# A new fixed order for the opening of a linear-attention and expert kernel, with fourteen wide operations on other engines

## The chip, the core and the metric

The kernel runs on one core of a Trainium2 chip. A core has five engines with a queue of instructions each: TensorE (PE: matrix products and transposes through its array), VectorE (DVE), ScalarE (ACT), GpSimd (POOL) and SyncE (SP, which here only issues transfers). Within a queue instructions start in order; between queues they are held together by semaphores. The metric is the device time of one execution in microseconds (us). The profile is one further execution, recorded by the hardware.

## The reference

```python
q_s = softmax(q, axis=-1)            # over the 64 features
k_s = softmax(k, axis=2)             # over the 576 positions
kv  = einsum('bhsd,bhse->bhde', k_s, v)
x   = einsum('bhsd,bhde->bhse', q_s, kv)   # 8 batches, 8 heads, 576 x 64
x   = x.transpose(0, 2, 1, 3).reshape(4608, 512)
h   = x @ w_in                       # 512 -> 2048
r   = maximum(h, 0)
out = (s * (r * r) + b) @ w_out      # 2048 -> 512
```

Everything is float32. The two large products run as sums of products of a high and a low part of each operand (`x` and `xl`, `gh` and `gl`, two parts of each weight), three products where one stood.

## The kernel before

The 4608 rows of x are cut in blocks of 512. A block is worked off in 16 steps, one for each 128 columns of `w_in`. Step t needs the weights w(t), which arrive as float32 and are split into two parts ("conversion", `conv_w`, L296 to L330): ACT L307, DVE L311, ACT L314, DVE L318, ACT L323, DVE L326, in that order, on 1024 columns for most weights and on two halves of 512 for some. Then PE does twelve matmuls of `h` (L1468), ACT takes the positive part (L1500), DVE squares it (L1523), ACT adds b and rounds to `gh` (L1525), DVE makes the rest `gl` (L1527), and PE does twelve matmuls of `acc` (L1548), eight with `gh` and four with `gl`, the first three of them two with `gh` and one with `gl`. The 16 weights are converted once, during the first block; later blocks find them in place.

Before the first step some attention must be done. Heads go in pairs u = 0, 1, 2, ...; the first four fill the 512 columns of block 0. For a pair of k (`k_stream`, L432): PE turns it (`kT`, L440), DVE takes the maximum (`km`, L443), ACT the exponentials (L448), PE turns it back (`kn`, L453), and an engine named by `KN_ON` copies it to where it came from (L455). PE then makes `kv` (L402), and DVE scales it to `kvf` (L420). For a pair of q (`q_stream`, L508): DVE takes the maximum (`qm`, L519), DVE or POOL subtracts it (L522, by `SUB_ON`), ACT exponentiates (L528), DVE sums and inverts (L531, L533), DVE or POOL multiplies (L538, by `MUL_ON`), PE turns the result (`qT`, L543), ACT or DVE copies it (L546, by `QF_ON`), PE makes `xp` (L553), ACT rounds it to the high part of x (L559), and DVE makes the low part (L563). k of later pairs goes another way (`k_pair`, L457: DVE L621 to L625, PE L629, DVE L632, PE L636, DVE L640, ACT L647). Some results share a PSUM bank in turn: `kn`, `qT` and `xp` of the first four pairs have two banks between them, `h` has one.

Nothing in this is scheduled on the chip. Each of these chains is a stream of `Op` entries with an engine, a cost and what it needs; a planner (`Order`) takes one entry after the other, and the order in which it takes them is the order in each engine's queue. In the opening the planner does not choose: two letters of `TURNS_TAKEN` name the stream that goes next. Where PE would have to wait by the planner's costs, `idle` (L1691) puts idle transposes (`unused`, L1702) in its queue. Transfers are issued from SP in that same order, over eight semaphores in rotation, so that an issue waits until the eighth transfer before it has landed.

Of the kernel before, what the change touches and what calls it, by code (L numbers as in the profile page):

```python
# [26 lines left out]
def attention_moe(ctx: ExitStack, tc: tile.TileContext, q, k, v, w_in, w_out, s, b, out):  # L27
    nc = tc.nc
    B, H, S, D = q.shape
    DM, FF = w_in.shape  # L30
# [107 lines left out]
    TURNS_TAKEN = (
        "aaaaababaaaaabaaabaWabaWabaQaWaWabaQaWaQabaWaXaWaQabaXaRaQaWauaRaXabaXaWabaRaXaba8aRaXabaXavabaRabauaSavabaua8avaSabauabaSaYaoauaSa8aYaZaTaS"
        "aqauaWaYaZaYaTaXaWaYaTaZbcaYaWaYaZa9aTaXaZbcaXaTawaZaYaZaXa9awaYaXawavaZbcaZa9adbcawavaYadaxaZavaeaYaxaeacaZbcaYawaZbcbcacayawbcbcaye1axbdbc"  # L140
        "bda4bcaxbda4aybdbcafaxafa4aybdbcbdbcaxagbdbcagaUbcbdbeaUaybebda4beazayapbeaAbda4e2a4bdazbea4bdaAazbdbeaAa4bfazbfbeaAbfa4ahaza4ahbfbea4aiaDaU"
        "azbeaibfbeaDaAbebfbeaDaAbgbfbgaDe3aBbgaCbfbgakaDaBbfakaCa1bgbfaDaBbfaCbfbgaEbhaBbgbhaCbgaBbhajaCbhajaBbgaCbhe4a1bgaFbha1bga1aEbgbha1biaEbhbi"
        "a1bia1aGbiaEa1bibhaUalbiaFbhalaGbibha0bibha0a1aUbibja0aEaUbjaFaEbjbjaGaUbiaFaJbibjbiaJaUambjbiaJamaGbkbjbkaUaJanbkaFbjanbaa5aJaFa5aGbkarbaaK"
        "babjaJbaa5bjaKataGbjaKbkbjaKaHblbkaKblaHbkaKe5blaHbkblaIaHbkblaIbkaHblaIbkaHblbkaIe6a0bmblaIbma0asa5aIbmaNa0a1a0aLa5bma1a5aNblbma5a1blbmaVa0"
        "bmblaVbmblaLa0bnbmaNa0aNaLbna0bnaMa0bnaNaLa5bmaMbnaNbma5aLa5bnaMbma5aLbmbnaMe7boaObnboaMaOaPboaMaOaPboa2aPaVaObnboaVbnboaPaVboa2bnaVa2bnboaV"
        "bpaOaPbpboaVaObpaVaPbpe8a2a3bobpa2a3bobpa2boa2bpboa3bqbpa3a2bpbqa3a2bqa3a3bqbpbqeQeQbpbqbpbqbpbqa3bbbqa3brbbcubrbbbbbrcva2cwbra2bqa2brcxbqbr"
        "a3brbqbrbqa3brbsa3bsa6bsa7bsdgbrbsdgbrbsbrePdgdQbrbsdgePbtdQeQbtbtbseQbtdgdRdgbsbtbsdRbta6bsa7bta6bsbtbua7btbua6a7a6bua7a6a7bua6a7bta6bubta7"
        "bua6btbudgbta6budQa6bvdQbvdQbvdQbvbubvdQbubvdQbubvbubwbvdgbwbwdgdsbwdsa6bvdtcza7bwdtbva7bwdRbvbwa7dRbveea7e9bwbxe9dRbxfhdRdQbxfhefcydRfhbxdR"
        "efcBfhbwefbxbwfhefbxbwefdSbxbwfhdSbxfhbyfabyfhcCbyfibyfifhfibxbyfibxfidQbybxfadQbybxcAdhdSbzbybzdRdhbzdSbzdhdSbydhbzfbdSfibyerbzfibydhbzdSdh"
        "byerbzbAdSerbAfibAererdibAfifjbzdibAbzfjbAbzfbdTbAbzcDfjdRdTbAbBdRbBdhbBfjdTdibBdSfjdibAdTbBfcbAbBfjdTbAdifjdTdibAbBfjbCbBesdTfjbCbBesfkbCes"  # L150
        "bCdTfkesbBdhesbCfcbBfkbCdhbBdufkdUbBbCdufkbDdUdifkdvbDbCdvbDdSbCbDfkcEdSbCbDfkbCdUfdflbCbDflfkbCdUbDbEfldUbDflegdUdTflbDbEcFegbEflegflbEdieg"
        "bDbEdUegbDdwbEbDfddwflbEdUbDdicGbFbEdxbFflfmbFdxdVbFfmdVfmetbFfebEetbFbEfmbFetbEbFetbEetfmbGcHfmdTbGfmbGdTbGdVehfebGdVdUeSbGbFdVeSbGehcJbFdV"
# [1606 lines left out]
```

## Time and profile before

| | us |
|---|---|
| median of 3 runs (lowest, highest) | 827.82 (827.21, 828.38) |
| the profiled execution | 828.27 |
| its span, first to last instruction | 826.5 |
| PE, DVE, ACT, POOL busy | 817.6, 673.3, 463.5, 205.3 |

The profiled execution took 1.8 us more than its span and lies 0.45 us above the median. The granted clock of TensorE is 1.0 throughout, the higher of its two levels. A busy share over the whole span says little here: the opening of some 36 us, the rest of the first block to about 110 us, and all that follows have different limits, and the rows below are taken from each.

### The profile page before, as it was taken

The numbers are of one execution on the slowest core, as the hardware profiler recorded it, in microseconds if no ns is written. First come the engines' busy times: TensorE is split into PE (matmuls) and PEld (weight loads), VectorE is DVE, ScalarE is ACT, GpSimd is POOL, SyncE is SP. The second block draws the span as 40 slices with busy tenths as digits, with TensorE's granted clock in tenths as the row PEclk, the third lists the DMA queues.
The fourth block names the chain that finished last, engine by engine and source line by source line (L and its number), as shares of the span: only waits on it lengthen the run. The fifth ranks groups of instructions, "written<-read, shape, count | busy, mean of one in ns | idle before, by whom it ended". The sixth has DMA issues, their size and how long they took to land.

```text
span 826.5 us, 12888 instructions
## 1 busy us (share of the span) xinstructions
PE 817.6 (99%) x4301; PEld 676.7 (82%) x4301; DVE 673.3 (81%) x1155; ACT 463.5 (56%) x768; POOL 205.3 (25%) x206
## 2 busy tenths in 40 slices
PE   8999999999999999999999999999999999999997
PEld 7688888888888888888888888888888888888886
DVE  6999956799899996978979978699969976656883
...
GB/s 267 319 375 318 164 70 110 151 228 191 218 179 198 168 170 205 214 177 144 203 241 163 242 149 149 231 264 283 276 253 325 251 156 214 203 182 187 90 18 73
DMA packets 217206, 165.64 MB, mean 200 GB/s; under 512 B 91444, under 2 KB 200500, under 8 KB 217140
## 3 DMA queue, kind: packets, MB, share of 16 engines
...
q10 hardware_dynamic: 5024, 0.98, 0.6%
...
## 4 chain that ended last, share of the span: by engine, by line
PE 96%; DVE 2%; issue 1%; ACT 0%; POOL 0%; POOLq 0%; ACTq 0%
PE acc L1548 27%; PE h L1468 26%; PE bankU L1104 11%; PE overX L1195 8%; PE bankV L1104 8%; PE overY L1195 5%; PE overZ L1195 5%; PE xp L830 2%; PE kv L402 2%; PE kT L440 1%; PE xp L553 1%; PE unused L1702 0%; PE bankU L1195 0%; DVE low L318 0%; DVE st L311 0%
## 5 line engine op out<-in xcount | busy, mean ns | idle before, releaser
L1468 PE MATMUL h<-x,w 128*128 128x512 f32 x960 | 238.2, 392 | 1.3 <-ACT r L1500 0.8
L1468 PEld LDWEIGHTS h<-x,w 128*128 128x128 f32 x960 | 177.9, 188 | 38.8 <-ACT r L1500 1.3
L1548 PE MATMUL acc<-w,gh 128*128 128x512 f32 x640 | 199.2, 392 | 0.0
L1548 PEld LDWEIGHTS acc<-w,gh 128*128 128x128 f32 x640 | 118.1, 188 | 23.5
L1548 PE MATMUL acc<-w,gl 128*128 128x512 f32 x320 | 125.1, 391 | 0.1
L1500 ACT ACTIVATE r<-h 128x512 f32<-128x512 f32 x80 | 47.9, 599 | 94.7 <-PE h L1468 94.1
L1104 PE MATMUL bankU<-w,ring 128*128 128x512 f32 x378 | 95.9, 389 | 0.0
L1104 PEld LDWEIGHTS bankU<-w,ring 128*128 128x128 f32 x378 | 70.9, 188 | 14.7
L1548 PEld LDWEIGHTS acc<-w,gl 128*128 128x128 f32 x320 | 60.1, 188 | 14.2 <-DVE gl L1527 0.9
L1104 PE MATMUL bankV<-w,ring 128*128 128x512 f32 x282 | 71.5, 389 | 0.0
L759 POOL TENSOR_TENSOR qe<-qe,qr 128x640 f32<-128x640 f32 x24 | 33.2, 1384 | 127.8 <-DVE qr L755 66.7
L1104 PEld LDWEIGHTS bankV<-w,ring 128*128 128x128 f32 x282 | 52.9, 188 | 11.0
L1514 DVE SCALAR_TENSOR_TENSOR h<-h,sb,r 128x512 f32<-128x512 f32 x47 | 35.3, 752 | 18.3 <-ACT r L1500 18.0
L742 POOL TENSOR_TENSOR area<-area,qm 128x640 f32<-128x640 f32 x24 | 31.2, 1300 | 74.3 <-DVE qm L740 45.4
L1516 ACT ACTIVATE gh<-h,sb 128x512 fp32r<-128x512 f32 x47 | 32.4, 690 | 28.6 <-DVE h L1514 28.5
L1195 PE MATMUL overX<-w,w 128*128 128x512 f32 (+1 forms) x177 | 40.5, 384 | 0.0
L1195 PEld LDWEIGHTS overX<-w,w 128*128 128x128 f32 x177 | 32.7, 188 | 6.5
L1518 DVE SCALAR_TENSOR_TENSOR gl<-h,sb,gh 128x512 fp32r<-128x512 f32 x47 | 34.7, 738 | 3.4 <-ACT gh L1516 3.2
L1510 DVE TENSOR_TENSOR gl<-r,gh 128x512 fp32r<-128x512 f32 x23 | 17.5, 762 | 15.6 <-ACT gh L1508 15.5
L927 DVE TENSOR_TENSOR S<-S 128x128 f32<-128x128 f32 x64 | 26.7, 418 | 0.7
L1195 PE MATMUL overZ<-gh,w 128*128 128x512 f32 x88 | 27.1, 389 | 0.0
L927 DVE TENSOR_TENSOR Z<-Z 128x128 f32<-128x128 f32 x64 | 25.2, 394 | 1.0
...
## 6 DMA issues: line engine op xcount, KB each, us to landing
...
```

What stands on the lines that cost most here:

```text
L742: nc.gpsimd.tensor_tensor(out=qt, in0=qt, in1=bc(qm, [P, 2, NT, D]), op=ALU.subtract)
L759: nc.gpsimd.tensor_tensor(out=qe_, in0=qe_, in1=qr, op=ALU.mult)
L927: eng.tensor_tensor(out=o, in0=x, in1=y, op=op)
L1104: nc.tensor.matmul(out_, w[:, a, c * P:(c + 1) * P], slot(k, c)[:, b_], start=k in (0, 1, 3) and n == 0, stop=n == 5, skip_group_check=True)
L1195: nc.tensor.matmul(out_, w[:, l], g[m][:, cols], start=k not in (2, 4) and p == begin_ and n == 0, stop=p == end_ and n == 2, skip_group_c ...
L1468: nc.tensor.matmul(hp_, w[:, j, c, :], x[:, c, :], start=(c == 0 and i == 0), stop=(c == NP - 1 and i == 2))
L1500: nc.scalar.activation(r, hp_, AF.Relu)
L1510: nc.vector.tensor_tensor(out=gl, in0=r, in1=gh.bitcast(F32), op=ALU.subtract)
L1514: nc.vector.scalar_tensor_tensor(out=hp_, in0=hp_, scalar=s_col, in1=r, op0=ALU.mult, op1=ALU.mult)
L1516: nc.scalar.activation(gh, hp_, AF.Identity, bias=b_col)
L1518: nc.vector.scalar_tensor_tensor(out=gl, in0=hp_, scalar=b_col, in1=gh.bitcast(F32), op0=ALU.add, op1=ALU.subtract)
L1548: nc.tensor.matmul(acc[blk, j // 2][:, j % 2], g[:, js], w_, start=(f == 0 and i == 0), stop=(f == NFC - 1 and i == 2))
```

## The change

Four tuples of engine names and the table of turns are different; no operation is added or left out.

```diff
-    KN_ON = ('ACT', 'DVE', 'ACT', 'DVE')
-    QF_ON = ('DVE', 'ACT', 'ACT', 'ACT', 'ACT', 'ACT', 'ACT', 'DVE')
+    KN_ON = ('ACT', 'ACT', 'ACT', 'ACT')
+    QF_ON = ('ACT', 'DVE', 'ACT', 'ACT', 'ACT', 'ACT', 'DVE', 'DVE')
...
-    SUB_ON = ('D', 'D', 'P', 'P', 'D', 'D', 'D', 'P')
-    MUL_ON = ('P', 'D', 'P', 'D', 'D', 'D', 'P', 'D')
+    SUB_ON = ('P', 'D', 'P', 'P', 'P', 'P', 'P', 'P')
+    MUL_ON = ('P', 'P', 'P', 'P', 'P', 'D', 'D', 'P')
...
-        "aaaaababaaaaabaaabaWabaWabaQaWaWabaQaWaQabaWaXaWaQabaXaRaQaWauaRaXabaXaWabaRaXaba8aRaXabaXavabaRabauaSavabaua8avaSabauabaSaYaoauaSa8aYaZaTaS"
+        "aaaaaaabaaabababababaWaQaQaWaWaWaQaQaXaXaXaXaXauauauaRaRauaRaRaSaQavauaRaXaWaWa8avavauaSaWaXaSaWa8aSabababababaTaZaYavaWavaZaZaSaZa8avaWaXaY"
...
```

The tuples have one entry for each k pair (`KN_ON`) or q pair. Two copies go from DVE to ACT (`KN_ON`, u = 1 and 3); one copy goes from DVE to ACT and two from ACT to DVE (`QF_ON`); four subtractions go from DVE to POOL (u = 0, 4, 5, 6); four multiplications go from DVE to POOL (u = 1, 3, 4, 7) and one from POOL to DVE (u = 6). The table covers about the first 150 us; from there on the order is as it was. What it does to the queues is shown at three places.

DVE before the third k pair (`km_2`), before the change; `z` is the scale of `kv`, `st_0` and `low_0` belong to the conversion of the first weights:

```order
L531 TENSOR_REDUCE qs_1_229<-qe_1_221 128x8 [waits Activation_49,Pool_49]
L408 TENSOR_SCALAR z_0_172<-z_0_172 128x2 [waits Activation_49]
L409 RECIPROCAL z_0_172<-z_0_172 128x2 [waits DVE_49]
L533 RECIPROCAL qs_1_229<-qs_1_229 128x8
L538 TENSOR_TENSOR qe_1_221<-qe_1_221,qs_1_229 128x512 [waits DVE_49]
L455 COPY area_87<-kn_1_244 128x640 [waits DMAHW7_49,DMAHW0_49,PE_49]
L311 TENSOR_SCALAR st_0_124<-st_0_124 128x512 [waits DMAHW1_49]
L311 TENSOR_SCALAR st_0_124<-st_0_124 128x512 [waits DMAHW4_49]
L443 TENSOR_REDUCE km_2_305<-kT_2_269 128x1 [waits PE_49]
```

and after it:

```order
L533 RECIPROCAL qs_1_191<-qs_1_191 128x8 [waits DVE_49]
L531 TENSOR_REDUCE qs_0_257<-qe_0_163 128x8
L533 RECIPROCAL qs_0_257<-qs_0_257 128x8 [waits DVE_49]
L408 TENSOR_SCALAR z_0_166<-z_0_166 128x2 [waits Activation_49]
L409 RECIPROCAL z_0_166<-z_0_166 128x2 [waits DVE_49]
L311 TENSOR_SCALAR st_0_124<-st_0_124 128x512 [waits DMAHW4_49]
L326 TENSOR_TENSOR w_0_253<-low0_0_193,w_0_253 128x512 [waits Activation_49]
L443 TENSOR_REDUCE km_2_265<-kT_2_239 128x1 [waits PE_49]
L519 TENSOR_REDUCE qm_3_323<-raw1_86 128x8 [waits DMAHW7_49]
L519 TENSOR_REDUCE qm_2_325<-raw1_86 128x8
L318 SCALAR_TENSOR_TENSOR low1_0_251<-st_0_124,low1_0_251 128x512 [waits Activation_49]
L420 TENSOR_TENSOR kvf_83<-kv_0_276,z_0_166 64x2x64 [waits DVE_49,PE_49]
```

The multiplication and the copy have left this stretch, and the conversion of the first weights has moved up, its last step L326 now ahead of `km_2`.

POOL in the opening and behind it, before the change (the small MEMSETs set one column):

```order
L522 TENSOR_TENSOR raw1_86<-raw1_86,qm_3_331 128x2x256 [waits DVE_49]
L526 MEMSET qe_3_372 128x8 [waits PE_49,Activation_49]
L538 TENSOR_TENSOR qe_2_357<-qe_2_357,qs_2_369 128x512 [waits DVE_49,Activation_49,Pool_49]
L584 TENSOR_TENSOR area_87<-area_87,qml_0_497 128x4x64 [waits DMAHW6_49,DVE_49]
L589 MEMSET ql_0_515 128x4 [waits PE_49,Pool_49]
L599 TENSOR_TENSOR ql_0_515<-ql_0_515,qsl_0_574 128x256 [waits DVE_49,Activation_49,Pool_49]
L526 MEMSET qe_5_758 128x8 [waits PE_49]
L526 MEMSET qe_4_833 128x8 [waits PE_49,Pool_49]
```

and after it, from L599 on:

```order
L599 TENSOR_TENSOR ql_0_495<-ql_0_495,qsl_0_528 128x256 [waits DVE_49,Activation_49,Pool_49]
L382 MEMSET area_87 64x4x64 [waits DMAHW2_49,Pool_49]
L383 MEMSET area_87 128x20 [waits DMAHW3_49,Pool_49]
L648 MEMSET area_87 64x2x64 [waits Activation_49,Pool_49]
L648 MEMSET area_87 64x2x64 [waits Activation_49]
L522 TENSOR_TENSOR area_87<-area_87,qm_4_658 128x2x256 [waits DMAHW3_49,DVE_49,Pool_49]
L526 MEMSET qe_4_701 128x8 [waits PE_49]
L522 TENSOR_TENSOR area_87<-area_87,qm_5_673 128x2x256 [waits DVE_49]
L526 MEMSET qe_5_770 128x8 [waits PE_49]
L538 TENSOR_TENSOR qe_4_701<-qe_4_701,qs_4_758 128x512 [waits DVE_49,Activation_49,Pool_49]
```

Behind L599, where POOL had only MEMSETs for a long stretch, three wide operations of u = 4 and 5 stand now.

PE from the last `kT` of the opening, before the change:

```order
L440 MATMUL kT_3_333<-ident_78,raw1_86 64x128
L553 MATMUL xp_0_354<-early_88,kvf_83 128x256 [waits DVE_49]
L553 MATMUL xp_0_354<-early_88,kvf_83 128x256
L543 MATMUL qT_1_363<-ident_78,qe_1_221 128x128 [waits Activation_49,Pool_49]
L543 MATMUL qT_1_363<-ident_78,qe_1_221 128x128 x3
L1468 MATMUL h_0_374<-x_0_353,w_0_317 128x512 [waits Activation_49]
L1468 MATMUL h_0_374<-x_0_353,w_0_317 128x512 [waits DVE_49]
L453 MATMUL kn_3_383<-ident_78,early_88 128x128 [waits DVE_49,Activation_49]
```

and after it:

```order
L440 MATMUL kT_3_312<-ident_78,raw1_86 64x128
L1702 MATMUL unused_112<-ident_78 128x128 x4
L553 MATMUL xp_0_343<-early_88,kvf_83 128x256 [waits DVE_49,Activation_49]
L553 MATMUL xp_0_343<-early_88,kvf_83 128x256
L543 MATMUL qT_1_346<-ident_78,qe_1_188 128x128 [waits Activation_49,Pool_49]
L543 MATMUL qT_1_346<-ident_78,qe_1_188 128x128 x3
L1702 MATMUL unused_112<-ident_78 128x128 x5
L453 MATMUL kn_3_379<-ident_78,early_88 128x128 [waits DVE_49,Activation_49]
L453 MATMUL kn_3_379<-ident_78,early_88 128x128 x4
L1702 MATMUL unused_112<-ident_78 128x128 x2
L553 MATMUL xp_1_387<-early_88,kvf_83 128x256 [waits DVE_49]
```

The first two matmuls of `h` have moved behind the second `xp`, and idle transposes stand in the gaps (59 in all, 47 before). SP issues the reload of k for the third pair of heads before the weights of step 2 now, where it stood behind those of step 4.

## Rows read from the trace of the kernel before

**Rows 1.** The page, part 1: busy us, share, instructions.

```profile
PE 817.6 (99%) x4301; PEld 676.7 (82%) x4301; DVE 673.3 (81%) x1155; ACT 463.5 (56%) x768; POOL 205.3 (25%) x206
```

**Rows 2.** Busy time by stretch: length, engines with counts, clock, DMA share, GB/s.

```profile
0.00:36.50 36.50, 31.99 (x286) 25.40 (x286) 28.86 (x52) 24.97 (x39) 9.39 (x27) 1.00 0.98 285
36.50:63.00 26.50, 26.48 (x119) 21.57 (x120) 25.63 (x36) 25.16 (x37) 1.06 (x3) 1.00 1.06 372
```

**Rows 3.** The chain that ended last, in order of time: start, us, what.

```profile
36.52 2.58 PE acc L1548 x10
39.11 2.72 PE h L1468 x12
...
62.15 2.72 PE h L1468 x12
...
75.77 1.32 PE kv L402 x40
```

**Rows 4.** PE in order of time: start, us, operation, idle time before it.

```profile
18.09 0.77 PE L453 MATMUL kn<-ident,early 128*128 128x128 f32 x5
...
22.66 0.74 PE L453 MATMUL kn<-ident,early 128*128 128x128 f32 x5
...
32.96 3.01 PE L1468 MATMUL h<-x,w 128*128 128x512 f32 x12 [0.78 <-ACT r L1500]
...
35.80 0.61 PE L1548 MATMUL acc<-w,gh 128*128 128x512 f32 x2
```

**Rows 5.** DVE in order of time, the opening.

```profile
10.20 1.19 DVE L522 TENSOR_TENSOR area<-area,qm 128x512 f32<-128x512 f32 x1
...
16.42 0.76 DVE L443 TENSOR_REDUCE km<-kT 128x1 f32<-128x576 f32 x1 [0.19 <-PE kT L440]
...
20.22 0.76 DVE L443 TENSOR_REDUCE km<-kT 128x1 f32<-128x576 f32 x1
...
22.55 0.50 DVE L408 TENSOR_SCALAR z<-z 128x2 f32<-128x2 f32 x1
...
31.51 1.22 DVE L326 TENSOR_TENSOR w<-low,w 128x1024 fp32r<-128x1024 f32 x1
32.64 0.69 DVE L311 TENSOR_SCALAR st<-st 128x1024 f32<-128x1024 f32 x1
33.24 0.74 DVE L1523 SCALAR_TENSOR_TENSOR r<-r,sb 128x512 f32<-128x512 f32 x1
...
34.23 1.22 DVE L318 SCALAR_TENSOR_TENSOR low<-st,low 128x1024 uint32<-128x1024 uint32 x1
35.37 1.10 DVE L1527 SCALAR_TENSOR_TENSOR gl<-r,sb,gh 128x512 fp32r<-128x512 f32 x1
```

**Rows 6.** POOL in order of time.

```profile
9.80 1.05 POOL L538 TENSOR_TENSOR qe<-qe,qs 128x512 f32<-128x512 f32 x1 [5.96 <-ACT early L448]
...
20.04 1.05 POOL L522 TENSOR_TENSOR raw<-raw,qm 128x512 f32<-128x512 f32 x1
...
21.98 1.05 POOL L538 TENSOR_TENSOR qe<-qe,qs 128x512 f32<-128x512 f32 x1
34.40 1.53 POOL L584 TENSOR_TENSOR area<-area,qml 128x256 f32<-128x256 f32 x1 [11.37 <-DVE qml L582]
...
505.18 4.07 POOL L1076 TENSOR_TENSOR stage<-stage 128x512 f32<-128x512 f32 x3 [4.87 <-DVE w L1047]
```

**Rows 7.** DVE in order of time, beside the last row of POOL.

```profile
508.03 1.77 DVE L1047 TENSOR_TENSOR w<-stage,w 128x512 fp32r<-128x512 f32 x1
```

**Rows 8.** Groups by line and shape, 0 to 160 us: busy us, mean ns.

```profile
L538 DVE TENSOR_TENSOR qe<-qe,qs 128x512 f32<-128x512 f32 x5 | 3.5, 692 | 0.2
L538 POOL TENSOR_TENSOR qe<-qe,qs 128x512 f32<-128x512 f32 x3 | 3.1, 1046 | 6.1 <-ACT early L448 6.0
L559 ACT CAST x<-xp 128x512 fp32r<-128x512 f32 x8 | 4.6, 586 | 6.5 <-PE xp L553 6.5
```

**Rows 9.** Loads of line 375, 0 to 90 us, from issue to landing.

```profile
DMA to landing us min/median/max: 3.1/6.5/9.1
```

More of the change, by code (lines that the diff above doesn't have):

```diff
@@ L138, in attention_moe @@
     TURNS_TAKEN = (
-        "aaaaababaaaaabaaabaWabaWabaQaWaWabaQaWaQabaWaXaWaQabaXaRaQaWauaRaXabaXaWabaRaXaba8aRaXabaXavabaRabauaSavabaua8avaSabauabaSaYaoauaSa8aYaZaTaS"
-        "aqauaWaYaZaYaTaXaWaYaTaZbcaYaWaYaZa9aTaXaZbcaXaTawaZaYaZaXa9awaYaXawavaZbcaZa9adbcawavaYadaxaZavaeaYaxaeacaZbcaYawaZbcbcacayawbcbcaye1axbdbc"
-        "bda4bcaxbda4aybdbcafaxafa4aybdbcbdbcaxagbdbcagaUbcbdbeaUaybebda4beazayapbeaAbda4e2a4bdazbea4bdaAazbdbeaAa4bfazbfbeaAbfa4ahaza4ahbfbea4aiaDaU"
-        "azbeaibfbeaDaAbebfbeaDaAbgbfbgaDe3aBbgaCbfbgakaDaBbfakaCa1bgbfaDaBbfaCbfbgaEbhaBbgbhaCbgaBbhajaCbhajaBbgaCbhe4a1bgaFbha1bga1aEbgbha1biaEbhbi"
@@ L143, in attention_moe @@
[L143 to L146, printed above, removed]
@@ L147, in attention_moe @@
-        "a3brbqbrbqa3brbsa3bsa6bsa7bsdgbrbsdgbrbsbrePdgdQbrbsdgePbtdQeQbtbtbseQbtdgdRdgbsbtbsdRbta6bsa7bta6bsbtbua7btbua6a7a6bua7a6a7bua6a7bta6bubta7"
-        "bua6btbudgbta6budQa6bvdQbvdQbvdQbvbubvdQbubvdQbubvbubwbvdgbwbwdgdsbwdsa6bvdtcza7bwdtbva7bwdRbvbwa7dRbveea7e9bwbxe9dRbxfhdRdQbxfhefcydRfhbxdR"
-        "efcBfhbwefbxbwfhefbxbwefdSbxbwfhdSbxfhbyfabyfhcCbyfibyfifhfibxbyfibxfidQbybxfadQbybxcAdhdSbzbybzdRdhbzdSbzdhdSbydhbzfbdSfibyerbzfibydhbzdSdh"
+        "aaaaaaabaaabababababaWaQaQaWaWaWaQaQaXaXaXaXaXauauauaRaRauaRaRaSaQavauaRaXaWaWa8avavauaSaWaXaSaWa8aSabababababaTaZaYavaWavaZaZaSaZa8avaWaXaY"
@@ new lines, in attention_moe @@
+        "aYaTaTaWaYaZaXaWaZaYa9aYaZaYawawaTaXbcaTaXaXaoabababababadadababaZa9aUa9aYbcacaZawaYaYaZaxaYaZaUacawawaYaxaZaxawa4bcbcbcbcbcbcaUbcbcaxa4a4ay"
+        "bcbcbdbdbdbda4ayaxbdaybdaAbdaxa4a4aUbcbcbcbebeaya4aUa4aUa4bdbdaAbcbebeayayazazbeaAa4azbeaAazapafagafaeagaqaiaeaiahahbdbdbdbfbfbea4bdbfbfbeaA"
+        "azbfaUaDaUaza0bfaAbfaEbfaEaDaUaBaBa1bebebebgbgbgbgbea0a0bgbfbabfbhbfbhbhbfbhbgaDa0aBaDa0bgbga0aBaDaEaBa1a1aDaBa1aFbhbgbgbgbibibiaCaEbhbabhaE"
+        "aCa1aFbha0bia0bhbgaCaFaCaEaCaCa5aGbaa5bibhbhbhbjbjbjbjbibibiaGaFa1bia5aFa1aFaGbjbjaGe3arajakakatamasalananajalambibibibibkbkbkbkaJbja0aVbjbj"
@@ new lines, in attention_moe @@
+        "bjaGaHa5a5aJaHbkbaaVa2bkbla1aVaHa1bkaVa3bjblblbla1bkaHaHaGa1a1a5aVbjblbkbkbla2a5a3a2aIa2blbka5a5bkbmbmbmbmaVaVaIa3bla5blblaVa3aIa2aIaJaJbmaJ"
+        "aVa5aHaJa2aKaKblbnbnbnbnbla0bbaLbmaLaKaKa2bmbmbmbmaIaIa0aKa0a3a3bnbnaKaNaLa3a2aOaLa2aNbnaLaNaLbnaMbmbmbobobmboboaOaMboaMaOa3bna3aNbbbobobobo"
+        "bbbbaMaNaNbnbpbpbpbnbnbpa2bpaMa2bobobobqbqbqbqboa2a3bpbpbpaPaOaOaObpaMbqaPaPbqa3bqbqaPa3bqaPcwcue6e2e1cvcxa7a6brbrbrbrbpbpbpbpbqbqbqbqbrbrbr"
+        "a6a7a7a6eQa6bra6aPbrdgdQbsbsbsbrbrbra6a6a6bsbrbsePdgdgeQdgbsdgbsbseQdQa7btbtbta6btbsbsbsbsa7btbtbtdQbtePdge4dgdQbtdRdga7dgbububububtbtbtbtbv"
@@ L150, in attention_moe @@
+        "bvbvdsbububua6a6a6budQa7a7bva7bububububvbvdtdtbva7a7a7bvdReedQdsdQbvbwbwbwbwbvbvbvbxbxbxefdRdRdRbwdRdRbwbwbwfhfhfhbxdQcydQcze8efcBeQe7e5fhbw"
+        "efbxbwfhefbxbwefdSbxaabwfhdSbxfhbyfabyfhcCdRbyfibyfifhfibxbyfibxfidQbybxfae9e9dQbybxcAdhdSbzbybzdRdhbzdSbzdhdSbydhbzfbdSfibyerbzfibydhbzdSdh"
         "byerbzbAdSerbAfibAererdibAfifjbzdibAbzfjbAbzfbdTbAbzcDfjdRdTbAbBdRbBdhbBfjdTdibBdSfjdibAdTbBfcbAbBfjdTbAdifjdTdibAbBfjbCbBesdTfjbCbBesfkbCes"
```

## The prediction

> **What bounds the kernel now.** I read the page's busy line first: PE is at 99% of the span [rows 1]. That alone says only that time can be won or lost where PE is not at useful work. The stretches show where: PE is short of its full time before 36.5 us, and from there to 63 us it is full while DVE and ACT run at 97% and 95% [rows 2]. So there are two limits. In the opening the chain of k and q work decides when the steps begin; behind it PE bounds, with DVE close on its heels. The chain in order of time confirms it: from 36.52 us on its pieces are PE's own, twelve matmuls in 2.72 us [rows 3]. PE's total of useful work is the same in both kernels, so the change in time is the change in two sums: how late the twelve matmuls of the second `h` begin (32.96 us before [rows 4]), and how long PE waits after that.
>
> **What a wide operation costs on either engine.** A multiplication of 128x512 takes 0.69 us on DVE, 0.60 from start to start, and 1.05 us on POOL [rows 8]. Beside that stands a lock. DVE's L522 at 10.20 took 1.19 us, because POOL's L538 ran from 9.80 to 10.85 [rows 5, 6]: it stood still until POOL was done and then took its usual 0.55 to 0.6. L408 at 22.55 stood until 23.05, POOL being busy from 21.98 to 23.03. It works the other way too: POOL's L584 at 34.40 took 1.53 us, because DVE's L318 held until 35.37, and then DVE's L1527 took 1.10 us behind it [rows 5, 6]. With several POOL operations in a row the two alternate: three took 4.07 us from 505.18, and DVE's L1047 at 508.03 took 1.77 us [rows 6, 7]. Reductions, and operations that read PSUM, are not held: `km` at 20.22 took its 0.76 us like that at 16.42, although POOL ran from 20.04 to 21.09 [rows 5, 6]. So an operation moved to POOL frees 0.60 us of DVE and can cost it up to 1.05.
>
> The Trainium skill (SBUF — State Buffer, Who interferes with whom) says that whoever starts first has the shared pair of ports for the whole instruction and the other fully blocks. The trace agrees; it matters for the tie below. The skill also advises VectorE for elementwise work, GpSimd being about twice as slow with two inputs (GPSIMD Engine Reference, Engine selection). Here the ratio is 1.05 to 0.60 or 0.69, 1.5 to 1.75; at the page's factor a lockout would last 1.2 to 1.4 us and the sum below would grow by about 1 us. The measured 1.05 is used.
>
> **First sum: the start of the steps.** Up to 14 us little differs: the loads are issued in the same order, `km` of the second pair comes at 11.8, and DVE's longer list has room. The first new lockout decides. DVE ends the inverse of u=0 at about 14.1; POOL's multiplication of u=0 follows 0.37 us after such an inverse starts, so at 14.36, and DVE's second L311 of weight 0 is due at 14.40. POOL has it by 0.04 us. Then DVE's L311 runs 15.36 to 15.74, POOL multiplies u=1 to 16.75, DVE's L326 (0.60) follows to 17.35, and `km` of the third pair stands behind it: 17.35, where it was 16.42 [rows 5]. That is 0.93 us late, and from `km` to `kn` it takes 1.67 us as before (16.42 to 18.09 [rows 4, 5]): `kn` at 19.0. PE has nothing to put there.
>
> Behind `km` come two reductions (1.2 us), L318 held by the subtraction of the next q (0.6 + 0.6), L420 (0.57), and L326 held again (0.3 + 0.6), so `km` of the fourth pair starts at about 22.05, where it was 20.22: 1.8 us late. Its exponentials end at 23.65. In ACT's queue the rounding of the first `xp` (0.5 us, [rows 8]) now stands behind them, and DVE's `xl` (0.6) behind that, at 24.85; only then is the PSUM bank free for the fourth `kn`, 24.9 instead of 22.66 [rows 4]: 2.2 us late. The copy of that `kn` is on ACT now, the next `kv` starts at 27.7, the last two `xp` end at 31.8 and the conversion of weight 1 (L326) starts at 33.4 instead of 31.51. ACT makes the positive part at 34.4, and the second `h` begins at 34.95: 2.0 us late. In that time PE also does the `kT` of the third pair early, 0.2 us that it need not do later. First sum: +1.8 us.
>
> What hides nothing here: the seven moves off DVE do shorten its list, by 3.3 us up to this point, but six POOL operations hold it for 3.9 us (0.96, 1.0, 0.6, 0.3, 0.7, 0.35) where before it was 0.6 + 0.35, and L621 to L625 of the third pair (1.4 us) are now ahead of the second `h`. The reload of k that L621 waits for is no term: issued behind the first `kv` at about 17.7, it lands after at most 9.1 us [rows 9], at 26.8, and DVE is there at 28.3.
>
> **Second sum: waits behind it.** I add up DVE's queue and PE's queue from the second `h` on, by spacing from start to start: 1024 columns of L318 or L326 1.14 us, of L311 0.60, L1523 and L1527 0.66 [rows 5], a reduction or half conversion 0.60, h and acc 2.72 each [rows 3], kv 1.32 [rows 3]. Check on the kernel before: up to the first `gl` DVE has 2.8 us to do, starts 0.28 us after PE (33.24 against 32.96), and is held 0.44 by POOL; PE wants `gl` 3.2 us after its start. It is 0.3 to 0.4 us late by this, and the trace has acc at 35.80 and its main run only from 36.52 [rows 3, 4]: they agree. Over the stretch from the second `h` to 62.15, where the seventh begins [rows 3], PE had 28.0 us of work in 29.2: 1.15 us of waiting.
>
> After: up to `gl` of step 5 DVE has 30.5 us in 44 instructions: eleven of 1.14, six L311 (3.6), L1523 and L1527 ten times (6.6), six of 0.60 for reductions and halves, and 4.2 of smaller ones and of L640 and L1510. PE wants that `gl` 32.3 us after its start (h six times 2.72, acc four and three quarters, kv 1.32, transposes 1.3). So there are 1.8 us to spare without POOL. But five POOL operations now stand in that stretch: L584 and L599 (0.6 and 0.5) as before, and the subtractions of u=4 and u=5 and the multiplication of u=4, 1.05 each, each followed on DVE by L318 or L326, which are held. That is 4.25 us: PE waits 2.5 us in all. Against 1.15 before: +1.3 us. Behind step 6 the spare time of DVE grows to over 5 us by the same sums, and nothing more is lost.
>
> Together +3.1 us on the profiled 828.27 (span 826.5, the 1.8 around it unchanged): 831.4. The median lies 0.45 under that execution, so I predict 827.82 + 3.1 = 830.9.
>
> **Rivals.**
> - The tie goes to DVE. L311 ends at 14.75, POOL's two multiplications come behind it, L326 gets in between, and `km` stands at 16.4. Every time above comes about 0.95 us earlier, first sum +0.85: 830.0. For it: 0.04 us is less than the spread of these starts. Against: the durations of neither engine change, and POOL has the earlier start.
> - Half the lockouts fall beside reductions or ACT's gaps. Second sum: DVE needs 30.5 + 2.1, PE waits about 0.5 less than before; first sum +0.85: about 828.4, no difference. For it: `km` and the reductions of rows 5 did pass beside POOL. Against: DVE's queue shows L318, L326 or L1523 next to nearly each of these operations.
> - Faster: POOL does not hold DVE in these places at all. `km` of the fourth pair starts 0.6 us earlier than before, the second `h` about 0.5 earlier, and the 1.15 us of waiting go: 826.0. It decides from the point where the sum of lockouts in the opening is under about 1 us, what it was before. Against it are the 1.19, 0.50 and 1.10 us of rows 5.
> - DVE's delays also hold ACT, which is as full (95% [rows 2]), and both wait on each other: another 1.2 us, 832.1.
>
> **How the numbers follow.** The forecast has 0.35, the tie 0.20, the fourth rival 0.05, half lockouts 0.24, faster 0.16. A measurement of this kernel tells 0.2%, 1.65 us, from no change, so slower starts at 829.5 and faster ends at 826.2. Slower holds 0.57 (the tie's 830.0 can fall short of it, a little more easily than half lockouts can exceed it, which takes 0.03), no difference 0.27, faster 0.16. The range reaches from 826.8, between half lockouts and faster, to 832.6, above the fourth; for the likeliest alone it is 829.6 to 832.2.
>
> **What would show it.** Right: in the profile after, DVE rows L311, L326 and L318 between 14 and 22 us that last 1.0 to 1.6 us beside POOL's; `km` of the third and fourth pair at 17.4 and 22; the second `h` at about 35; idle time of PE before `acc` on DVE `gl` between 50 and 75 us of 2 us or more. Wrong: `km` at 16.4, or the second `h` before 33; DVE rows of usual length beside POOL; a granted clock below 1.0; or a load that DVE or ACT waits for.

## The result and the profile after

| | us |
|---|---|
| before, median of 6 (lowest, highest) | 827.80 (827.21, 828.38) |
| after, median of 6 | 833.82 (831.94, 835.10) |
| ratio, 95% interval | 1.0070 (1.0055 to 1.0085) |
| after, repeated later: ratio | 1.0073 (1.0060 to 1.0085) |

The changed kernel is about 6 us slower. The forecast was 830.9: slower is right, the size is half of it, and the time lies above the range. Four executions of 1174 to 2678 us, two of the kernel before and two of the one with both late places mended, are left out of every figure here. The profiled execution of after is the slowest of the six, 835.10 us with a span of 833.2; that is 6.8 us above the 828.27 of the profiled one of before.

I read the stretches first, now cut so that the whole loss can be placed. After, by stretch: length, then busy time and count of PE, PEld, DVE, ACT, POOL; clock, DMA share, GB/s.

```profile
0.00:36.50 36.50, 30.68 (x294) 25.58 (x295) 26.77 (x47) 24.39 (x39) 12.37 (x27) 1.00 0.97 299
36.50:63.00 26.50, 26.50 (x156) 21.89 (x155) 26.31 (x34) 24.60 (x35) 6.10 (x10) 1.00 0.94 297
63.00:125.00 62.00, 60.70 (x314) 49.75 (x313) 51.02 (x88) 51.88 (x86) 7.94 (x12) 1.00 0.56 168
125.00:220.00 95.00, 91.61 (x500) 74.54 (x500) 72.77 (x148) 45.58 (x81) 20.21 (x27) 1.00 0.69 191
```

The two later stretches of before in the same view:

```profile
63.00:125.00 62.00, 62.00 (x356) 51.10 (x354) 49.89 (x86) 52.02 (x86) 6.06 (x13) 1.00 0.56 182
125.00:220.00 95.00, 95.00 (x536) 78.79 (x535) 79.83 (x164) 45.94 (x81) 22.10 (x28) 1.00 0.66 178
```

PE's busy time is short of before by 1.31 us in the opening [rows 2], by 1.30 from 63 to 125 us, and by 3.39 from 125 to 220 us: together 6.0 of the 6.8. PE also has 0.8 us more of busy time in all (818.4 against 817.6 [rows 1], the added idle transposes among it). More than half of the loss lies in the last of these stretches, where the prediction had nothing.

Which waits they are, PE in order of time says (start, us, operation, then the idle time before it and what ended it):

```profile
15.10 1.31 PE L440 MATMUL kT<-ident,raw 128*64 128x128 f32 x20 [1.08 <-DMA raw<-in_k_dram]
34.62 3.02 PE L1468 MATMUL h<-x,w 128*128 128x512 f32 x12 [0.71 <-ACT r L1500]
65.23 3.04 PE L1468 MATMUL h<-x,w 128*128 128x512 f32 x12 [1.30 <-ACT r L1500]
148.85 0.66 PE L610 MATMUL xpl<-early,kvf 128*128 128x64 f32 x4 [1.29 <-ACT early L606]
150.69 0.44 PE L603 MATMUL qTl<-ident,ql 128*128 128x128 f32 x2 [0.43 <-POOL ql L599]
194.80 0.50 PE L1548 MATMUL acc<-w,gl 128*128 128x512 f32 x1 [1.38 <-DVE gl L1510]
```

The second `h` is 1.66 us later than before [rows 4]; for before the same view shows no wait of PE from 36.5 to 300 us. So there are three places behind the opening: near 65, near 149 and near 195 us (there a second, shorter one of 0.28 follows at 200.81).

**Near 65 us** the positive part that `h` waits for, L1500, stands in ACT's queue behind L307 of a later weight, and that one waits for DVE's L326, which stood still beside POOL's multiplication of u = 4 (POOL; DVE by shape, 61 to 64.2 us, with busy us and mean ns; ACT):

```profile
61.13 1.29 POOL L538 TENSOR_TENSOR qe<-qe,qs 128x512 f32<-128x512 f32 x1 [2.58 <-DVE qs L533]
...
L326 DVE TENSOR_TENSOR w<-low,w 128x1024 fp32r<-128x1024 f32 x1 | 2.1, 2062 | 0.0
...
63.54 1.16 ACT L307 ACTIVATE low<-st 128x1024 int32<-128x1024 uint32 x1 [0.77 <-DVE w L326]
64.58 0.59 ACT L1500 ACTIVATE r<-h 128x512 f32<-128x512 f32 x1
```

L326 took 2.06 us on its 1024 columns, against 1.22 before [rows 5].

**Near 149 us** PE waits for ACT's copy L606, whose input PE had ready at 136.6 us (`qTl`, L603, 136.25 and 0.38 long). ACT in order of time:

```profile
145.91 0.74 ACT L729 ACTIVATE area<-area 128x640 f32<-128x640 f32 x1 [5.25 <-DVE area L687]
146.55 0.58 ACT L1500 ACTIVATE r<-h 128x512 f32<-128x512 f32 x1
147.96 0.69 ACT L1516 ACTIVATE gh<-h,sb 128x512 fp32r<-128x512 f32 x1 [0.83 <-DVE h L1514]
148.54 0.26 ACT L606 COPY early<-qTl 128x128 f32<-128x128 f32 x1
```

Here L606, a step of `q_left`, stands behind L729, the exponentials of a later pair of k, and L729 stands for 5.25 us waiting for DVE's L687. That one waits in turn for a transfer: the maxima of a pair of k go out to memory (L679) and come back spread over all partitions (L683). DVE:

```profile
145.05 0.82 DVE L687 TENSOR_TENSOR area<-area,misc 128x640 f32<-128x640 f32 x1 [2.72 <-DMA misc<-maxima]
```

In the kernel before, L606 of this pair ran at 142.31 and L729 at 150.21, in the opposite order.

**Near 195 us** it is SP's queue. DVE stands ahead of the `gl` that PE wants (rows left out between):

```profile
189.27 0.42 DVE L667 TENSOR_REDUCE sb<-misc 128x8 f32<-128x256 f32 x1 [1.04 <-DMA maxima<-sb]
...
194.10 0.64 DVE L1510 TENSOR_TENSOR gl<-r,gh 128x512 fp32r<-128x512 f32 x1
```

SP of after (issues; SPq is its queue):

```profile
160.57 1.10 SPq L889 DMA_DIRECT2D aset<-w  x2
...
167.59 1.30 SPq L889 DMA_DIRECT2D aset<-w  x2
...
169.70 1.60 SPq L889 DMA_DIRECT2D aset<-w  x2
...
183.05 0.41 SPq L679 DMA_DIRECT2D maxima<-sb  x1
```

and of before:

```profile
173.78 0.34 SPq L679 DMA_DIRECT2D maxima<-sb  x1
```

In after the small transfer of maxima, whose data DVE had ready at 178.2, is issued 4.9 us later, at 183.05. Three of the eight groups of copies of weights for the later blocks (`a_copies`, L889 and L890) have been put ahead of it; before had issued all eight by 107.5 us, after only five by 137.5. So the order isn't the old one again from about 150 us on, as was said ahead of the prediction: the two tables differ up to place 738, and these three groups stand at places 692, 696 and 697, issued from 160 to 172 us.

**The opening** shows the signs that the prediction named, but not all of their effect. DVE after, the answer to [rows 5]:

```profile
14.13 0.92 DVE L311 TENSOR_SCALAR st<-st 128x512 f32<-128x512 f32 x1 [0.35 <-DMA st<-in_moe_w_out_dram]
15.34 1.16 DVE L326 TENSOR_TENSOR w<-low,w 128x512 fp32r<-128x512 f32 x1 [0.28 <-ACT w L323]
16.45 0.76 DVE L443 TENSOR_REDUCE km<-kT 128x1 f32<-128x576 f32 x1
17.93 1.28 DVE L519 TENSOR_REDUCE qm<-raw 128x8 f32<-128x512 f32 x2 [0.72 <-DMA raw<-in_q_dram]
19.13 1.16 DVE L318 SCALAR_TENSOR_TENSOR low<-st,low 128x512 uint32<-128x512 uint32 x1
...
21.77 0.76 DVE L443 TENSOR_REDUCE km<-kT 128x1 f32<-128x576 f32 x1
```

POOL after, beside it, the answer to [rows 6]:

```profile
13.72 2.23 POOL L538 TENSOR_TENSOR qe<-qe,qs 128x512 f32<-128x512 f32 x2 [8.04 <-DVE z L408]
18.70 1.04 POOL L522 TENSOR_TENSOR raw<-raw,qm 128x512 f32<-128x512 f32 x1 [2.75 <-DVE qm L519]
...
19.74 1.45 POOL L522 TENSOR_TENSOR raw<-raw,qm 128x512 f32<-128x512 f32 x1
```

DVE's L326 and L318 of 512 columns take 1.16 us beside POOL's wide operations, instead of the 0.68 that they took in before at 19.50 and 17.09. But `km` of the third pair starts at 16.45, where it was 16.42 [rows 5]. These starts can't be compared as they stand, because each execution begins with its first loads, which land at different times: the first `kn` starts at 8.93 here, at 9.70 in before, and at 8.63 to 10.03 in the other profiles. Counted from it, the third `km` is 7.52 us behind against 6.72, and the second `h` 25.69 against 23.26. Part of that isn't the order's: a load of k let PE wait 1.08 us at 15.10, a load of q DVE 0.72 us at 17.93.

### The profile page after: what moved, and what is told of

Its sections match the earlier page's. It is cut to its first block, busy times and chain, and to the rows that moved or that the text cites. A ratio compares the mean times of both kernels' runs of the same rounds, so it can differ in the third digit from the quotient of the medians.

```text
span 833.2 us, 12911 instructions
## 1 busy us (share of the span) xinstructions
PE 818.4 (98%) x4313; PEld 677.4 (81%) x4313; DVE 671.6 (81%) x1147; ACT 462.8 (56%) x769; POOL 215.6 (26%) x213
## 4 chain that ended last, share of the span: by engine, by line
PE 86%; DVE 6%; DMA 5%; issue 2%; ACT 1%; SPq 0%; ACTq 0%; POOL 0%; DVEq 0%; POOLq 0%
PE acc L1548 22%; PE h L1468 21%; PE bankU L1104 10%; PE overX L1195 8%; PE bankV L1104 8%; PE overY L1195 5%; PE overZ L1195 5%; PE kv L402 2%; PE xp L830 2%; DMA maxima<-sb 1%; DMA raw<-in_q_dram 1%; DVE w L326 1%; DVE low L318 1%; PE xp L553 1%; DMA area<-in_q_dram 1%
## 5 line engine op out<-in xcount | busy, mean ns | idle before, releaser
L1500 ACT ACTIVATE r<-h 128x512 f32<-128x512 f32 x80 | 48.0, 600 | 93.1 <-PE h L1468 91.1
L763 DVE STREAM_TRANSPOSE area<-qe 128x640 f32<-128x640 f32 x24 | 20.1, 836 | 7.9 <-POOL qe L759 7.9
```

The source lines that it names most:

```text
L763: nc.vector.transpose(out=tb, in_=qe.rearrange("p h t n r -> p (h t n r)"))
L1500: nc.scalar.activation(r, hp_, AF.Relu)
```

## The experiments

Each kernel below was timed in five rounds beside the kernel before; its ratio is to those runs. Most edits only move turns of the new table: on line 243 the table becomes a list, and pairs (from, to) are moved in it. The numbers are places in the table, which has 3557 turns; each pair counts from the list as the pair ahead of it has left it.

**The copies earlier.** The three late groups of `a_copies` go to where the others are issued:

```diff
-            turns = iter([...])
+            turns = [...]; [turns.insert(b, turns.pop(a)) for a, b in ((692, 545), (696, 546), (697, 547))]; turns = iter(turns)
```

> The changed kernel with three turns moved: the copies of converted weights to DRAM (a_copies 4, 6 and 7, nine issues on SP's queue), which it issues from 160 to 172 us, go right behind the loads of line 576 at 115 to 116 us, where the DMA queues are nearly empty. In the changed kernel PE waits 1.38 us at 194.80 and 0.28 us at 200.81 for gl of line 1510, behind DVE's L667 that waited until 189.27 for the transfer of the maxima, which SP issued only at 183.05 though its data was ready at 178.2. Theory A (SP's queue sets these two waits: it carries some 6 us more issues between 155 and 190 us than before): both waits go, PE is 1.66 us earlier, 832.2 us, at least 1.2 us below the changed kernel. Theory B (the round trip of the maxima itself, 5 to 6 us, sets them, whenever it is issued): less than 0.4 us is gained, 833.5 to 834.

Measured 831.00 (830.59 to 831.59), ratio 1.0035 (1.0022 to 1.0048). PE has no wait at 195 or 201 any more; those at 64.19 (1.31), 147.66 (1.14) and 149.50 (0.43) are still there.

**The q_left work earlier.** ACT's L606 goes ahead of L729, and DVE's L594 and L596 and POOL's L599 of the next pair go ahead of DVE's L687: four turns, as (619, 615), (636, 600), (641, 618), (642, 619).

> The changed kernel with four turns moved: ACT's copy of the turned leftover q of pair 2 (L606, now behind L729, L1500 and L1516) directly behind the transpose that it copies, and the sum, inverse and multiplication of the leftover q of pair 3 (L594, L596, L599) ahead of DVE's L687, which waits for the transfer of the maxima until 145.05. Theory A (the wait of 1.29 us at 148.85 and that of 0.43 at 150.69 come from the place of these small operations in the queues of ACT and DVE alone): both go from the trace. What the whole gains is open by A: if SP's queue, which sets the later wait of 1.66 us at 194.80 and 200.81, runs on its own clock, that wait grows by what was won, 833.0 to 833.8; if it moves with PE, 832.1. Theory B (ACT and DVE are held by the transfer of the maxima anyway, so that the wait only moves to the next h or gl): PE still waits 1.5 us or more between 140 and 160 us, 833.8.

Measured 831.62 (830.48 to 832.14), ratio 1.0040 (1.0027 to 1.0053). The wait for L606 is gone. A shorter one takes its place, 0.94 us at 148.47 before L603, for ACT's L345; near 195 us 0.65 and 0.29 remain.

**The old engines under the new table.** The four tuples of before:

```diff
-    KN_ON = ('ACT', 'ACT', 'ACT', 'ACT')
+    KN_ON = ('ACT', 'DVE', 'ACT', 'DVE')
...
-    MUL_ON = ('P', 'P', 'P', 'P', 'P', 'D', 'D', 'P')
+    MUL_ON = ('P', 'D', 'P', 'D', 'D', 'D', 'P', 'D')
```

> The new table of turns with the old engines: the four tuples KN_ON, QF_ON, SUB_ON and MUL_ON of the kernel before. Theory A (the order is what costs: the waits at 65, 149 and 195 us are made by the table, and the engines cost only in the opening): the second h comes 0.5 to 1 us earlier than its 34.62, the wait of 1.30 us at 65.23 stays at 0.8 or more, since three operations of 0.60 us come back to DVE where 2.3 us of standing still go, and those at 149 and 195 us stay as they are: 832.5 to 833.5. Theory B (POOL's hold on DVE is what costs, as predicted): the second h at 33.2 or earlier and no wait at 65 us, 830.5 to 831.

Measured 839.02 (838.19 to 839.32), ratio 1.0129 (1.0115 to 1.0144): 5 us slower still than after. PE in order of time shows where, rows left out:

```profile
30.21 0.63 PE L543 MATMUL qT<-ident,qe 128*128 128x128 f32 x4 [1.77 <-DVE raw L455]
...
38.57 3.02 PE L1468 MATMUL h<-x,w 128*128 128x512 f32 x12 [0.70 <-ACT r L1500]
```

The second `h` is 4 us later than in after: a copy that is DVE's again holds PE in the opening. The late waits are there all the same, 1.05 and 0.43 us at 152.37 and 154.21, 0.87 and 0.29 at 197.97 and 203.99, so they come with the table and not with the engines. The one near 65 is not; 0.92 us before `qT` on DVE's L538, at 71.91, stands in its place.

**The old table with the new engines** (the reverse edit, in the kernel before).

> The old table of turns with the new engines: the four tuples of the changed kernel in the kernel before. Theory A (the order costs, the engines little): the second h up to 0.7 us later than 32.96 and nothing behind it, 827.8 to 828.8. Theory B (POOL's hold on DVE costs): the opening loses 1 to 2 us and DVE's queue from 36 to 63 us another 1 us, 829.8 to 831.

Measured 828.86 (828.25 to 829.48), ratio 1.0008 (0.9998 to 1.0017): no difference that these runs can tell. The second `h` starts at 32.14. One new wait shows, 0.53 us before `acc` on DVE's `gl` at 53.94, of the kind that the prediction's second sum is about. So under the old table the new engines cost nothing that can be measured; the loss comes with the new table.

**The changed kernel again**, as a control for its spread.

> The changed kernel once more, unchanged, as the measure for the runs beside it. In its first profile two loads were waited for (PE 1.08 us at 15.10 for k of the third pair, DVE 0.72 us at 17.93 for q of the second pair) and the second h came at 34.62; in two kernels with the same opening it came at 33.57 and 33.53. Theory A (the landing of these loads differs from run to run and is worth 1 us): the second h at 33.5 to 34.7 and a time of 832 to 834.5, spread over 2 us or more. Theory B (the opening is as steady as that of the kernel before): within 0.6 us of 833.8.

Measured 833.90 (832.94 to 835.35), ratio 1.0073 (1.0060 to 1.0085). In this profile no load is late in the opening, and the second `h` starts at 33.88; the waits near 65 (1.29), 148 (1.16 and 0.43) and 193 (0.21 and 0.28) are there.

**Both late places mended** (the first two edits together).

> The moves of e1_copies and e2_left together. Theory A (the waits at 149 and 195 us are two separate places in the queues, of ACT and of SP): against the changed kernel beside it 1.66 + 1.72, less the 0.9 us that stayed at 148.47 in e2_left, so 2.5 us less, about 831 minus what the opening gives. Theory B (one backlog behind both, so that taking away one takes away what the other would give): no more than e1_copies alone, 1.7 us.

Measured 830.2 (829.44 to 831.12), ratio 1.0028 (1.0016 to 1.0039), against 1.0073 for the unmended kernel in the same rounds: 0.45%, 3.7 us. What PE still waits for behind the opening:

```profile
64.28 3.04 PE L1468 MATMUL h<-x,w 128*128 128x512 f32 x12 [1.23 <-ACT r L1500]
148.26 0.41 PE L603 MATMUL qTl<-ident,ql 128*128 128x128 f32 x2 [0.52 <-ACT misc L345]
```

**L621 to L625 behind the second h**, as (104, 141), (116, 141), (131, 145): the prediction had counted 1.4 us of DVE's time for them ahead of it.

> The changed kernel with DVE's L621 to L625 of the third k pair (1.85 us from 26.36 to 28.74 in e1_copies) and PE's transpose of them moved behind gl of step 0 and behind the second h. Theory A (DVE is full without a gap from 20 to 65 us, and the wait of 1.3 us at 65 is the end of its backlog): the second h comes 1.2 to 1.8 us earlier, the waits behind it grow by the same, and the time stays within 0.4 us of the changed kernel beside it. Theory B (the opening and the wait at 65 us are two separate losses): 1.2 to 1.8 us less.

Measured 835.08 (834.89 to 836.01), ratio 1.0087 (1.0074 to 1.0101). The second `h` comes at 33.50, 0.4 us earlier than in the control; counted from the first `kn` (8.63) that is 24.87 us against 23.85 in the control, with a wait of 0.51 us for a load of k in it, so nothing was gained. Then PE waits for what was put off:

```profile
38.02 0.44 PE L629 MATMUL kT<-ident,misc 128*128 128x128 f32 x2 [1.51 <-DVE misc L625]
```

DVE now stands idle for 0.92 and 0.63 us, ahead of L420 and L563, about where those 1.4 us of work were: they fitted into gaps that the chain of k leaves on DVE anyway.

**The q work of u = 4 and 5 later**, behind the conversions of weight 10 (18 pairs, the first of them (216, 321)), to see whether it makes the wait near 65.

> The changed kernel with the work on q of u=4 and u=5 (DVE: two maxima, two sums, inverses and a multiplication, some 3.0 us; POOL: two subtractions and a multiplication, beside which DVE stood still for some 2.3 us) put behind the conversions of weight 10, some 15 us later. Theory A (DVE's backlog ends in the wait at 65.23): that wait goes, 1.0 to 1.3 us less than the changed kernel beside it, unless a transpose of q waits between 72 and 85 us. Theory B (the wait at 65 us is ACT's, whose read of h stands behind the conversion of weight 10, whatever DVE has to do): 0 to 0.3 us less.

Measured 836.29 (835.69 to 837.32), ratio 1.0103 (1.0087 to 1.0118). The wait near 65 is gone, but the work has to be done before block 0 ends, and PE waits three times for it, 2.74 us in all, with the granted clock at half behind that (82 to 85 us):

```profile
78.14 0.50 PE L1548 MATMUL acc<-w,gl 128*128 128x512 f32 x1 [0.85 <-DVE gl L1527]
80.20 0.66 PE L543 MATMUL qT<-ident,qe 128*128 128x128 f32 x4 [0.84 <-POOL qe L538]
81.91 1.61 PE L1468 MATMUL h<-x,w 128*128 128x512 f32 x3 [1.05 <-ACT r L1500]
...
83.00:84.00 1.00, 1.00 (x6) 0.50 0.00 0
```

The last line is PE by stretch, with the clock of 0.50 behind the count.

**Two turns of the opening put off by five places**, as (84, 89) twice: ACT's L307 and DVE's L311 of weight 1, so that ACT's copy of the fourth `kn` comes ahead of that L307.

> The changed kernel with ACT's copy of the fourth kn (L455, 24.72 in a1_again) put ahead of the first L307 of weight 1 (23.65, 1.16 us), as the order of the kernel before has it, and DVE's L311 of that weight behind it. Theory A (the opening of the new order is late because the k chain stands in ACT's queue behind a conversion: e6_kpair showed that DVE's own work is not it): kv of the second pair 0.8 to 1.2 us earlier than 26.09 us, the second h 0.5 to 1.0 earlier than 33.88, and, if the wait at 64.5 does not grow, as much less than the changed kernel's 833.9: 833.0 to 833.4. Theory B (another entry of the queues, the copy of qT by ACT behind L314 at 26.73, is the next to hold): the second h less than 0.3 us earlier, no difference in time.

Measured 834.40 (832.64 to 835.70), ratio 1.0073 (1.0061 to 1.0084): no gain. The second `h` stands at 33.40, inside what the unmended order of the opening shows (33.24 to 33.88 where no load was late). Near 148 us the wait for L606 was 2.10 us in this profile, and then the clock fell, of which more below.

**The positive part of step 5 earlier in ACT's queue**, as (267, 266), (276, 275), (276, 283), (278, 290): ahead of L307 of weight 9, behind which it stood.

> The changed kernel with two places changed around 64 us: ACT's read of h of step 5 (L1500) goes ahead of the L307 of weight 9, which waits 0.77 us for DVE, and DVE's L1523 and L1527 of step 5 go ahead of L318 of weight 8, with ACT's L323 of that weight behind. Nothing is taken off any engine. Theory A (the wait of 1.3 us at 64.50 comes from the order of the two queues; step 5 is needed sooner than weight 8): the wait goes and no new one of more than 0.3 us comes before 100 us: 832.6 to 832.9 beside the changed kernel's 833.9. Theory B (DVE and ACT have too much work before this point, as e7_delay showed, where the wait went when work was taken away and came back as 2.7 us at 78 to 82): it comes back before 100 us: 833.5 to 834.2.

Measured 834.74 (834.15 to 835.73), ratio 1.0079 (1.0066 to 1.0092). The wait near 65 goes, and a longer one comes six microseconds later, with a slow `h` behind it:

```profile
71.15 4.63 PE L1468 MATMUL h<-x,w 128*128 128x512 f32 x12 [1.84 <-ACT r L1500]
```

So that wait isn't one bad place in ACT's queue. With the run that put the q work off it speaks for DVE and ACT having too much to do up to there, so that whichever goes first, the other is missed; neither run shows that by itself.

**All four edits** (the last two and the two late places).

> The moves of e1_copies, e2_left, e8_copy and e9_step5 together in the changed kernel; no operation changes engine. If the new table loses only at these four places of the queues, 3.3 us of e5_both and the gains of the other two add up: 828.5 to 829.5, within 0.2% of the kernel before. If they share one backlog: as e5_both, 830.6.

Measured 832.03 (830.79 to 832.29), ratio 1.0042 (1.0029 to 1.0055): worse than the two late places alone, by the wait of 1.76 us at 71.38 that it takes from the edit of step 5 and by the half clock behind it (the twelve matmuls of that `h` took 4.27 us).

**The old table, new engines for the opening only** (u = 4 to 7 as before), in the hope of the earlier `h` without the wait at 53.94.

> The kernel before, its table unchanged, with the new engines for the opening alone (KN_ON, QF_ON of u=0 and 1, SUB_ON of u=0, MUL_ON of u=1 and 3); u=4 to 7 as before. In e4_table the second h came at 32.14 instead of 32.96, and two waits took that back, 1.02 us before it instead of 0.78 and 0.53 at 53.94. Theory A (the wait at 53.94 is the lateness of DVE, whose total of work from 36 to 63 us is what it was, so an earlier start is given back): 827.6 to 828.4, no difference from the kernel before. Theory B (that wait came from the subtractions of u=4 and u=5 on POOL): no wait at 54 us, 0.5 to 0.8 us less than before, 827.2.

Measured 828.27 (827.61 to 829.48), ratio 1.0003 (0.9994 to 1.0012): no difference. The second `h` starts at 32.84, and the wait on `gl` (0.44 at 54.36) is there all the same. From the first `kn` to the second `h` it is 23.3 to 23.5 us in this kernel (9.50 to 32.84) and in the kernel with the old table and all of the new engines (8.69 to 32.14); the earlier `h` there was an earlier first load.

**The table in pieces.** In the next four the engines are those of after. A piece of one table comes first; then the turns that are left follow in the other's order. The kernels hold the finished table; this sketch says how it is put together:

```python
first = ...   # the first 160 turns of one table (about 37 us), or 536 (125 us), or 512 (109 us)
left = Counter(first)
for turn in other:
    if left[turn] > 0: left[turn] -= 1
    else: first.append(turn)
```

The new opening, then the old order:

> The engines of the changed kernel throughout; its first 160 turns (to the start of acc of step 0, about 37 us), and from there the turns of the kernel before, in its order. Theory one, each stretch has its own loss: the opening alone is kept, second h at 33.4 to 34.6, no wait at 65, 149 or 195: 1.0 to 1.7 us over the kernel before, about 829.5. Theory two, the opening leaves DVE and ACT in arrears and the later waits follow from that: waits of about 1.3 us or more come between 50 and 75 us although the order there is the old one, 831 or more.

Measured 828.70 (828.13 to 830.14), ratio 1.0010 (1.0001 to 1.0018). The waits near 65, 149 and 195 are not there; the only one left behind 36 us is 0.27 at 47.32.

```profile
33.45 3.02 PE L1468 MATMUL h<-x,w 128*128 128x512 f32 x12 [0.71 <-ACT r L1500]
...
36.76 0.39 PE L1548 MATMUL acc<-w,gl 128*128 128x512 f32 x1
```

The second `h` is 0.5 us later than before, and the `acc` with the first `gl` at 36.76 only 0.24 later than the 36.52 of [rows 3]: the kernel before lost time there that this one doesn't. Counted from the first `kn` (9.46 here, 9.70 before) they are 0.73 and 0.48 later. The opening costs 0.1%, 0.8 us, with an interval of 0.1 to 1.5 us.

The new order to 125 us, then the old:

> The changed kernel's first 536 turns (to about 125 us), then the old order; all eight groups of copies for the other blocks are issued at the join or before 160 us, and ACT L606 has its old place. Theory one: opening and the wait near 65 are kept, the two late waits go: about 2.7 us over the kernel before, 831, like the version with both late places mended (830.6). Theory two, the late waits are what is left of arrears: a wait of over 1 us remains between 130 and 200 us, 832 or more.

Measured 829.57 (829.20 to 830.33), ratio 1.0018 (1.0009 to 1.0027). By the waits, only the one near 65 is left, and nothing behind it:

```profile
64.42 3.02 PE L1468 MATMUL h<-x,w 128*128 128x512 f32 x12 [1.34 <-ACT r L1500]
```

The reverse of the first, the old opening and the new order from there:

> The reverse: the first 160 turns of the kernel before, then the changed kernel's order, with the changed kernel's engines. Theory one: second h at 32.2 to 33.0, then the wait near 65 (1.3 us), those near 149 (1.7) and near 195 (1.7) as in the changed kernel: 832 to 833. Theory two: with the opening of old the waits behind it go, at least the one near 65: 828 to 830.5.

Measured 836.34 (835.57 to 836.99), ratio 1.0099 (1.0085 to 1.0113). The joint itself costs something: PE waits 2.60 us at 40.07 for L625, which the old opening had not begun, and the clock falls behind that. The time can't be read for that, the places can. A wait of 1.02 us before `h` stands at 68.09, 0.90 and 0.43 near 152, and 0.27 at 201.63. So the wait near 65 comes under the old opening too; it belongs to the order behind it.

The old order to 109 us, then the new:

> The first 512 turns of the kernel before (to about 109 us, with all eight groups of copies issued), then the changed kernel's order. Theory one: second h at about 32.5, no wait at 65, the wait near 149 (1.3 to 1.7) is there, since it is a place in ACT's queue, the one near 195 is not, since no copies are left to issue: about 1.6 us over the kernel before, 829.8. Theory two: no wait behind 110, because nothing is in arrears: no difference from the kernel before, 828.2.

Measured 834.32 (833.35 to 835.74), ratio 1.0077 (1.0063 to 1.0091). Here too the joint spoils the time: two waits of 0.87 and 1.76 us, at 113.72 and 116.12, for q work that the new order takes to be done, with the half clock behind the second. Near 151 us 0.17 and 0.43 remain, and nothing near 195, all copies having been issued early. What the late places would cost in an otherwise undisturbed old order is left open.

## Why the prediction was wrong

The kernels in pieces give the loss by stretch, in ratios to the kernel before: 0.10% (0.8 us) up to 37 us, another 0.08% (0.7 us) to 125 us, and the other 0.52 to 0.55% (4.3 to 4.6 us) behind it. The intervals of these ratios are about 0.1% to either side, so the first two parts are small and known only roughly; the third is clear.

**The step that failed** is the end of the second sum: "Behind step 6 the spare time of DVE grows to over 5 us by the same sums, and nothing more is lost." That DVE has time to spare there is right; the sum was blind to the two queues that decide. ACT's L606 stands behind an operation that waits 5.25 us by way of DVE and a transfer, and the transfer of maxima stands behind copies in SP's queue. Neither ACT nor DVE is short of time, they are busy for 45.58 and 72.77 of 95 us, and yet PE loses 3.39 us of that stretch. Both places could be read from the order of the instructions on ACT and SP up to 200 us; I had read it only where PE was already known to be tight. That they are the cause is shown by taking them away: 1.0073 becomes 1.0035, about 3 us, with the copies alone earlier, 1.0040 with L606 and its neighbours alone, 1.0028 with both. The two gains don't add up, and 0.8 us of what stands behind 125 us is left by the ratios; the 0.52 us at 148.26 are part of it, the rest is open.

The gain of both, 3.7 us, is also more than PE's waits there: they add up to 3.38 us in the profile of after and to only 2.08 in that of the repetition, less the 0.52 that stay. In three of the five executions of the repetition the mean granted clock was 0.998 (833.90, 834.83 and 835.35 us), in the other two 1.0 and 0.999 (833.31 and 832.94). That fits a fall of the clock behind a longer wait, as in the last section, which mending would save too; no profile of after has one, so it isn't shown.

**The first sum** was too large: +1.8 us predicted, 0.8 measured for the opening by itself, and the second `h` at 33.24 to 33.88 where no load was late, not at 34.95. The rival of the tie had +0.85 and is the nearer one. In after a late load (0.35 us at 14.13) put POOL ahead of DVE's L311. In the new opening with the old order behind it nothing was late, L311 got through at its usual length, and only L326 was held:

```profile
14.22 0.41 DVE L311 TENSOR_SCALAR st<-st 128x512 f32<-128x512 f32 x1
14.88 1.19 DVE L326 TENSOR_TENSOR w<-low,w 128x512 fp32r<-128x512 f32 x1 [0.25 <-ACT w L323]
16.00 0.74 DVE L443 TENSOR_REDUCE km<-kT 128x1 f32<-128x576 f32 x1
```

Counted from the first `kn`, the third `km` is 6.54 us behind it here against 6.72 before, the fourth 11.03 (at 20.49) against 10.52, the fourth `kn` 13.13 (at 22.59) against 12.96, and the second `h` 23.99 against 23.26. So the terms that were too large are the 0.93 us at the third `km`, the 1.8 at the fourth and the 2.2 at the fourth `kn`, which came to -0.2, 0.5 and 0.2; most of the 0.73 us of the second `h` arises behind that `kn`. The sum was also wrong to count L621 to L625 as delay: putting them off brought nothing. What makes the 34.62 of the profile is in part the late loads of that execution.

**The second sum** to 125 us, +1.3 predicted, is 0.7 measured: one wait of 1.2 to 1.3 us on `h`, not several on `gl`, where the kernel with the new opening alone has 0.27 us at 47.32. (PE's terms, as the sum lists them, add up to 31.9 us and not to 32.3; that would have made it 0.4 larger still. By their own terms the rivals of half the lockouts and of faster come to 828.2 and 826.2, not to 828.4 and 826.0; neither came true.) Its reason, that POOL's operations eat up DVE's spare time, fits the rows: L326 took 2.06 us beside POOL's L538 at 61.13, and L318 as much at 57.52 beside POOL's L522 at 57.05, each 1.22 otherwise. The wait goes when the q work is put off, and isn't there with the old engines either. But the engines alone don't make it: with the old order they cost nothing that can be measured.

**The lockouts** are real and were priced rightly one by one, 1.16 and 1.19 us for operations of 0.68. The Trainium skill (SBUF — State Buffer, Who interferes with whom) calls the shared ports an exclusive lock, and these rows agree. The error was to carry them to the end of the kernel as a cost of the moves: with all the new engines in the old order the time is the same within what these runs tell (1.0008), with those of the opening alone too (1.0003), and under the new order taking the moves back costs 5 us. What left DVE seems to have paid for them; no run separates the two.

The fourth rival, DVE's delays holding ACT for another 1.2 us, came nearest with 832.1. The wait near 65 us is of its kind, L307 waiting for L326 and L1500 behind it; but the time that was missing from the forecast lies behind 125 us and has another reason, so that it came near was luck.
